# Queries pooled earlier on GpSimd in the first batches, and the first keys turned on TensorE ahead of the first queries

## The chip, the core and the metric

The kernel runs on one core of a Trainium2 chip. The metric is the device time of one execution in microseconds. A core has five engines that run side by side, each through its own list of instructions in order: TensorE (PE, matrix products), VectorE (DVE), ScalarE (ACT), GpSimd (POOL) and SyncE (SP, which here only issues DMA transfers). They meet at semaphores. Before the change three runs took 1130.13, 1131.37 and 1131.44 us, median 1131.37.

## What is computed

The reference has two parts, all in float32. The first is attention for 8 batches of 8 heads over 1152 positions of 64 features, with queries averaged in pairs:

```
q_pool = q.reshape(B, H, S // 2, 2, D).mean(axis=3)      # 576 queries a head
scores = 1/sqrt(D) * q_pool @ k.T                         # 576 x 1152
attn   = exp(scores - rowmax);  attn /= sum(attn) + 1e-9
attn_out = attn @ v
```

The second takes the 4608 rows of 512 features that come out and sends each through one of 8 experts (two products of 512x1024 and 1024x512 with a relu between them), chosen by the largest of 8 gate logits, and scales the result by the gate's probability.

## The kernel before, in words

Attention is worked off in 32 pairs of heads: pair n is head pair hp = n mod 4 of batch b = n div 4 (b and hp both from 0). Each pair has two units, one for each half of its 576 pooled queries. A unit goes through these steps:

- Scores (`scores`, line 631): 9 key chunks, four 64x64 matmuls each, into a bank of PSUM. DVE takes each bank out into a tile `s` (line 635) and keeps the chunk's extreme values (`mx`, reduced at lines 659 and 662, with a small matmul at line 656 between them).
- Exponentials on ACT (line 666), in place in `s`.
- Folds on POOL (`chunk_sum`, line 726): `s` has 9 chunks of 576 columns; POOL adds chunks 0 to 2 and 3 to 5 (1728 columns), adds 6 to 8, and then the third of the three sums to the first (576 columns). So a unit costs POOL two long additions and a short one. The last unit of a batch has one long addition alone (line 722). TensorE sums the folded tiles of a pair's two units with a product against ones (line 716).
- Values (`values`, line 770): products of `s` with the values `vn` into a bank `pa`, taken out by ACT and DVE (lines 776 and 777).

Before a pair's first scores there are its loads and turns (`load_pair`). SP issues the loads at line 490: keys `kp`, queries `qn`, values `vn`, each as four DMAs of 144 KB (128 bytes of an element at a time for keys and queries). POOL adds neighbouring queries, `qp<-qn` (line 520, the pooling). DVE turns the pooled queries into `qT` (line 533, two halves) and the keys into `kT` (line 529, three pieces). There is one `qn` buffer and one `qp` buffer, so the next pair's `qn` load waits until POOL has pooled the one before, and the pooling until DVE has turned the one before. There are two `kp`, three `vn`, four `s` and three `fold` buffers.

The very first pair is different (`first_pair`): its queries and keys are loaded with whole rows, TensorE turns them by products with an identity matrix (`cross_k`, line 589, and `cross_q`, line 595, which pools as it goes), and ACT copies the turned keys and DVE the first half of the turned queries out of PSUM (line 582).

The order of the instructions on each engine is fixed when the program is built. Every step is given to a planner (`Flow`) with an engine, an estimate of its time and a key; the planner runs an event list with one free time for each engine, and takes on each engine the step with the lowest key among those that are ready. A pair's keys start from `key` = 40 times its number. The pooling has `key + K_POOL` with `K_POOL = -28`, a fold `key + K_SUM` with `K_SUM = 25` plus 20 for each half and 20 more. DMAs are steps of the plan as well, with an estimated time from issue to landing (`move`). Once built, an engine keeps to the order whatever really comes late: a step whose data is not there holds all that stands behind it on its engine.

After pair 3's keys and values SP also issues, once, stores that fill scratch memory: `empty_lists`, `gate_weights` and `last_rows` (lines 400 to 412). Attention takes the span up to about 670 us, the experts the rest.

Of the kernel before, what the change touches and what calls it, by code (L numbers as in the profile page):

```python
# [14 lines left out]
ALU = mybir.AluOpType  # L15
# [17 lines left out]
K_POOL = -28  # L33
# [230 lines left out]
def kernel(  # L264
# [170 lines left out]
    def heads(t, b, hp):  # L435
        t = t[b] if isinstance(b, int) else t[bass.ds(b, 1)].rearrange("o h s d -> (o h) s d")
        return t[2 * hp:2 * hp + 2]
# [7 lines left out]
    def turn_ns(n):  # L445
        return 67 + 1.042 * n

    def pool(n):
        return 140 + 2.125 * n
# [10 lines left out]
    def tile_of(o, kind, shape, dt=F32, bufs=None, name=None, pool=None):  # L460
        return hold_of(kind, lambda h: (pool or o.wk).tile(shape, dt, **h.own(name or kind, bufs)))
# [10 lines left out]
    def done(*steps):  # L472
        return [s for s in steps if s is not None]

    def load_pair(o, f, key, b, hp):

        x = Pools()
        x.later, x.late = {}, hp
        opening = not o.exact and b == 0 and hp == 0
        if opening:  # L480
            return first_pair(o, f, key, x)

        kp = tile_of(o, "kp", [P, NQD * NC, BL], bufs=2, pool=o.ld)
        qn = tile_of(o, "qn", [P, NJ, NB, 2, BL], pool=o.ld)
        x.vn = vn = tile_of(o, "vn", [P, 2, NC, D], bufs=3, pool=o.rt)
        qp = tile_of(o, "qp", [P, NJ, NB, BL], pool=o.ld)
        x.kT = kT = tile_of(o, "kT", [P, NC * P], bufs=KT_BUFS, pool=o.kq)
        x.qT = qT = tile_of(o, "qT", [P, NQ], bufs=KT_BUFS, pool=o.kq)

        load = lambda out, src: nc.sync.dma_start(out=out, in_=src)  # L490
        rows = NQD * NC

        def quarters(t, src, n0=0, n1=rows):

            for h in range(2):
                for i in range(D // BL):
                    g = (h * D // BL + i) * BL
                    load(t[g:g + BL, n0:n1], src[h][:, i * BL:(i + 1) * BL].rearrange("(p n) d -> p n d", p=BL)[:, n0:n1])

        def k_part(n0, n1, ns, move, after=()):  # L500
            return f.carry("SP", ns, lambda: quarters(kp.t, heads(k, b, hp), n0, n1), key + K_LOAD, after, [kp], move)

        start = not o.exact and b == 0 and hp == 1

        def q_part(n0, n1, ns, move):
            return f.carry("SP", ns, lambda: quarters(qn.t.rearrange("p j b t d -> p (j b t) d"), heads(q, b, hp), n0, n1),
                    key + K_LOAD, (), [qn], move, 3000 if first and hp == 2 else 0)

        js = [slice(half * NJ // 2, (half + 1) * NJ // 2) for half in range(2)]
        first = not o.exact and b == 0  # L510
        paced = first and hp < 3
        move = 4400 if first else 2600
        k0 = k_part(0, rows, 1900, move, done(not start and o.asked or None))
        cuts = [(0, rows // 2), (rows // 2, rows)] if start else [(0, rows)]
        q0 = [q_part(n0, n1, 1900 // len(cuts), move // len(cuts)) for n0, n1 in cuts]
        vb = heads(v, b, hp).rearrange("h (p b c) d -> b p h (c d)", b=NQD, c=NC)
        x.v = f.carry("SP", 1900, lambda: [load(vn.t[i * BL:(i + 1) * BL].rearrange("p h c d -> p h (c d)"), vb[i]) for i in range(NQD)],
                      key + K_V, done(q0[-1] and q0[-1][9][0]), [vn], 2200 if first else move)
        parts = js if start else [slice(0, NJ)]
        q1 = [f.add("POOL", pool(NJ * QP // len(parts)), lambda j=j: nc.gpsimd.tensor_tensor(  # L520
            qp.t[:, j], qn.t[:, j, :, 0, :], qn.t[:, j, :, 1, :], ALU.add), key + K_POOL, done(got), [qn, qp])
            for j, got in zip(parts, q0)]
        q1 = [q1[0], q1[-1]]
        o.asked = q0[-1] and q0[-1][9][0]
        key += K_PIECE + (START if start else 0)
        x.k, x.q = {}, {}

        def turn_k(c0, n):
            nc.vector.transpose(kT.t.rearrange("p (c b i) -> p b c i", b=NQD, i=BL)[:, :, c0:c0 + n],  # L529
                                kp.t.rearrange("p (b c) d -> p b c d", b=NQD)[:, :, c0:c0 + n])  # L530

        def turn_q(half):
            nc.vector.transpose(qT.t.rearrange("p (j b i) -> p j b i", b=NB, i=BL)[:, js[half]], qp.t[:, js[half]])  # L533

        def turned(half):
            x.q[half] = done(f.add("DVE", turn_ns(HQ), lambda: turn_q(half), key + 7 * half, done(q1[half], paced and o.pace or None), [qT, qp]))
            o.turned.extend(x.q[half])

        turned(0)
        for c0 in range(0, NC, TURN):  # L540
            n = min(TURN, NC - c0)
            e = f.add("DVE", turn_ns(n * P), lambda c0=c0, n=n: turn_k(c0, n), key + 2 + c0 / 2, done(k0, paced and o.pace or None), [kT, kp])
            o.turned.extend(done(e))
            x.k.update((c, done(e)) for c in range(c0, c0 + n))
        turned(1)
        return x

    def first_pair(o, f, key, x):
# [8 lines left out]
        qn = lambda u: flat()[:QP, 2 * NC * D + u * 4 * QP * 2:2 * NC * D + (u + 1) * 4 * QP * 2].rearrange("p (h n d) -> p h n d", h=2, d=D)  # L557
# [5 lines left out]
        def load_q(u, gs, eng):  # L563
            for g in gs:
                eng.dma_start(out=qn(u)[g * BL:(g + 1) * BL].rearrange("p h n d -> p h (n d)"),
                                    in_=heads(q, 0, 0).rearrange("h (i u g n) d -> u g i h (n d)", i=BL, u=2, g=NB)[u, g])
# [3 lines left out]
        q0 = [done(f.carry("SP", 500, lambda: load_q(0, (0,), nc.sync), at + 1, (), [raw], 350),  # L570
                   f.carry("ACT", 900, lambda: load_q(0, range(1, NB), nc.scalar), at + 1, (), [raw], 700))]
# [7 lines left out]
        def turned(fn, ns, n, to, key, after, eng, cost, copy):  # L579
            pt = score_banks(o)  # L580
            t = f.add("PE", ns, lambda: fn(pt.t[:, 0, :n.stop - n.start]), key, after, [pt, raw], COLS)
            made = done(f.add(eng, cost(n.stop - n.start), lambda: copy(to.t[:, n], pt.t[:, 0, :n.stop - n.start]), key, done(t), [pt, to]))
            o.turned.extend(made)
            return made
# [6 lines left out]
        def cross_q(u, to):  # L591
            for m in range(NB):
                for t in range(2):
                    for h, up in enumerate(both):
                        nc.tensor.matmul(to.rearrange("p (g m i) -> p m g i", g=NB, i=BL)[up, m], qn(u)[:, h, 2 * m + t], ident[:QP, :QP],
                                         start=t == 0, stop=t == 1, tile_position=(0, up.start))

        def turn_k(c0, n, at, got, behind=()):
            made = turned(lambda to: cross_k(c0, n, to), 400 * n, slice(c0 * P, (c0 + n) * P), kT, key + at, done(got, *behind), "ACT", act, nc.scalar.copy)
            x.k.update((c, made) for c in range(c0, c0 + n))  # L600

        def turn_q(u, at, got, behind=()):
            side = ("ACT", act, nc.scalar.copy) if u else ("DVE", dve, nc.vector.tensor_copy)
            x.q[u] = turned(lambda to: cross_q(u, to), 1600, slice(u * HQ, (u + 1) * HQ), qT, key + at, [*got, *behind], *side)

        turn_k(0, FIRST, 0, k0[0])
        turn_q(0, -1, q0[0])
        x.later = {1: lambda m: turn_k(FIRST, TURN, 0, k0[1], m), 4: lambda m: turn_k(FIRST + TURN, TURN, 0, k0[1], m),
                   7: lambda m: turn_q(1, 0, q0[1], m)}
        return x  # L610
# [193 lines left out]
    def attend(o, f, key, b, hp, xT, sm, summed):  # L804
        x = load_pair(o, f, key, b, hp)
        outs = []
        end = not o.exact and hp == NHP - 1 and b == B - 1
        for half in range(2):
            at = key + 20 * half
            s, r = scores(o, f, at, x, half, EXPS)  # L810
            summed += chunk_sum(o, f, at + 20, s, r, b, hp, half, sm, summed[-1:])
            outs.append(values(o, f, at + 10 - (40 if end and half else 0), x, s, r, hp, half, xT))
        return done(*outs)
# [592 lines left out]
    with ExitStack() as cm, ExitStack() as units, ExitStack() as pairs:  # L1406
        o, m = open_attention(False, cm, pairs, units), Pools()
# [19 lines left out]
        for b in range(B):  # L1427
# [10 lines left out]
            key = PAIR * (b * NHP + NHP)  # L1438
# [45 lines left out]
    with tc.If(more > 0):  # L1484
        again = nc.values_load(stab[0:1, 1:2], min_val=0, max_val=1,
                               skip_runtime_bounds_check_because="a comparison's result")
        with tc.If(again > 0):
            reset_state()
            empty_lists()
            with ExitStack() as cm:  # L1490
                o = open_attention(True, cm, cm, cm)
# [16 lines left out]
        with ExitStack() as cm:  # L1508
            o, m, f = Pools(), Pools(), Flow()
# [41 lines left out]
```

## Time and profile before

| | |
|---|---|
| median of three runs | 1131.37 us (1130.13 to 1131.44) |
| profiled execution | 1125.42 us, of which its span 1123.6 us |
| granted TensorE clock, mean | 0.999 |
| TensorE busy | 1109.8 us (99%) |
| VectorE busy | 875.9 us (78%) |
| GpSimd busy | 857.6 us (76%) |
| ScalarE busy | 619.7 us (55%) |
| DMA, mean over the span | 141 GB/s |

The profiled execution has 1.82 us around its span. Times in the rows below are counted from the start of the span. A row of the timeline begins with when the instruction (or the first of xN equal ones) started and how long it (or all of them together) took, and ends, where the engine stood idle just before, with that idle time and what ended it, in square brackets.

### The profile page before, as it was taken

Reading aid. Unit: us, or ns where it says so; the run is one execution under the profiler, and the core shown is the slowest. Engines: PE = TensorE matmul, PEld = TensorE weight load, DVE = VectorE, ACT = ScalarE, POOL = GpSimd, SP = SyncE. Lnnn points to the kernel's source line nnn. Section 1 sums busy time; section 2 is a strip of 40 time slices with the busy share of each in tenths; the row PEclk is TensorE's granted clock in tenths of the full one; section 3 lists DMA queues with packets and bytes.
Section 4 is the critical chain, followed back from the end, with each engine's and each line's share of the span. In section 5 each row is a group of like instructions: output and inputs, shape, how many; then the busy total and the mean of one; then the engine's idle time right before and its main releaser. Section 6 shows DMA issues by size and latency. Waiting matters only on the chain.

```text
span 1123.6 us, 32966 instructions
## 1 busy us (share of the span) xinstructions
PE 1109.8 (99%) x13317; PEld 797.1 (71%) x13317; DVE 875.9 (78%) x2244; ACT 619.7 (55%) x835; POOL 857.6 (76%) x488
## 2 busy tenths in 40 slices
PE   9999999999999999999999999999999999999997
PEld 5565565565565565655655558998889989899996
DVE  7898998988989979989989969755555665677761
ACT  3756565666556656566557465544444445555551
POOL 3899999999999899998999854576666655456511
PEclk9999999999999999999999999999999999999999
DMA  9876757537738738637635159865555666577640
GB/s 158 141 139 111 129 86 124 113 66 122 115 66 132 112 64 139 114 66 134 112 63 99 27 169 243 232 188 166 164 174 176 201 192 191 191 233 255 229 158 30
DMA packets 387502, 158.06 MB, mean 141 GB/s; under 512 B 302694, under 2 KB 357762, under 8 KB 387342
## 3 DMA queue, kind: packets, MB, share of 16 engines
q1 hardware_dynamic: 376718, 134.91, 54.4%
q0 software_dynamic: 10464, 20.78, 5.9%
q8 instruction: 106, 1.74, 0.8%
q14 instruction: 54, 0.44, 0.2%
q10 hardware_dynamic: 160, 0.20, 0.1%
HBM read 135.02 MB, written 22.07 MB: 140 GB/s over the span
## 4 chain that ended last, share of the span: by engine, by line
PE 66%; DVE 15%; issue 6%; POOL 5%; DMA 4%; SPq 2%; ACT 0%; POOLq 0%; DVEq 0%; ACTq 0%
PE py L1384 17%; PE ph L1354 16%; PE pa L770 15%; PE st L631 14%; DVE s L635 8%; POOL fold L726 3%; DMA vn<-in_v_dram 2%; SPq L490 2%; DVE kT L529 2%; PE st L716 2%; DVE row L937 1%; PE st L709 1%; POOL qp L520 1%; DVE qT L533 1%; DMA x_runs<-row 1%
## 5 line engine op out<-in xcount | busy, mean ns | idle before, releaser
L666 ACT ACTIVATE s<-s,bias 128x1152 f32<-128x1152 f32 (+1 forms) x320 | 351.3, 1152 | 166.4 <-DVE bias L662 156.7
L635 DVE TENSOR_SCALAR_CACHE_REDUCE s<-st 128x576 f32<-128x576 f32 x576 | 415.1, 748 | 32.4 <-PE st L631 21.7
L631 PE MATMUL st<-qT,kT 64*64 64x288 f32 x4608 | 359.9, 407 | 4.6 <-DVE s L635 2.8
L770 PE MATMUL pa<-s,vn 64*64 64x288 f32 x4608 | 351.4, 404 | 1.0 <-DVE xT L777 0.8
L631 PEld LDWEIGHTS st<-qT,kT 64*64 64x64 f32 x4608 | 166.9, 133 | 121.3 <-DVE s L635 37.3
L770 PEld LDWEIGHTS pa<-s,vn 64*64 64x64 f32 x4608 | 174.6, 133 | 104.3 <-DVE xT L777 10.8
L726 POOL TENSOR_TENSOR fold<-s 128x1728 f32<-128x1728 f32 x55 | 213.0, 3875 | 5.5 <-ACT s L666 3.1
L726 POOL TENSOR_TENSOR fold<-fold,s 128x1728 f32<-128x1728 f32 x55 | 213.0, 3876 | 0.9
L1354 PE MATMUL ph<-xh,w1h 128*128 128x248 f32 (+4 forms) x512 | 155.6, 304 | 0.2 <-DVE hl L1364 0.2
L1354 PE MATMUL ph<-xh,w1l 128*128 128x248 f32 (+4 forms) x512 | 154.6, 302 | 0.0
L1354 PE MATMUL ph<-xl,w1h 128*128 128x248 f32 (+4 forms) x512 | 154.6, 302 | 0.0
L1226 DVE TENSOR_TENSOR w2l<-raw,w2h 128x1024 fp32r<-128x1024 f32 x64 | 78.3, 1223 | 80.6 <-ACT w2h L1311 76.8
L1083 POOL DMA_INDIRECT xr<-x_runs,ix x76 | 97.5, 1283 | 51.6 <-issue 26.0
L1384 PE MATMUL py<-w2h,hh 128*128 128x512 f32 x328 | 128.1, 391 | 0.0
L1384 PE MATMUL py<-w2h,hl 128*128 128x512 f32 x328 | 127.8, 390 | 0.0
L1384 PE MATMUL py<-w2l,hh 128*128 128x512 f32 x328 | 127.8, 390 | 0.0
L1393 POOL DMA_INDIRECT out_dram<-y,rec x41 | 43.9, 1071 | 85.7 <-ACT y L1401 70.3
L1362 ACT ACTIVATE hh<-ph 128x372 fp32r<-128x372 f32 (+4 forms) x100 | 49.3, 493 | 108.2 <-PE ph L1354 108.0
L1354 PEld LDWEIGHTS ph<-xh,w1h 128*128 128x128 f32 x512 | 96.4, 188 | 2.6 <-issue 0.9
L1354 PEld LDWEIGHTS ph<-xl,w1h 128*128 128x128 f32 x512 | 96.4, 188 | 0.7
L1354 PEld LDWEIGHTS ph<-xh,w1l 128*128 128x128 f32 x512 | 96.4, 188 | 0.0
L1364 DVE SCALAR_TENSOR_TENSOR hl<-ph,hh 128x372 fp32r<-128x372 f32 (+4 forms) x100 | 55.6, 556 | 51.1 <-ACT hh L1362 50.8
(230 smaller groups left out, 1339.1 us busy)
## 6 DMA issues: line engine op xcount, KB each, us to landing
raw<-in_moe_w_dram SPq DMA_DIRECT2D x128, 512.0 KB
kp<-in_k_dram SPq DMA_DIRECT2D x124, 144.0 KB
vn<-in_v_dram SPq DMA_DIRECT2D x124, 144.0 KB
qn<-in_q_dram SPq DMA_DIRECT2D x120, 144.0 KB
x_runs<-row SPq DMA_DIRECT2D x96, 99.0 KB
xr<-x_runs,ix POOLq DMA_INDIRECT x76, 4.3
x_runs<-empty SPq DMA_DIRECT2D x4, 297.0 KB
xq<-x_runs,ix POOLq DMA_INDIRECT x52, 3.3
```

The lines of the kernel that those rows point to most:

```text
L631: nc.tensor.matmul(pt.t[to, h, :HQ], x.kT.t[up, c * P + i * D:c * P + (i + 1) * D], x.qT.t[up, cols], start=True, stop=True, tile_position ...
L635: nc.vector.tensor_scalar(s.t[:, c], pt.t[:, :, :HQ], -SCALE, None, op0=ALU.mult, op1=ALU.min, accum_out=mx.t[:, c:c + 1],)
L666: nc.scalar.activation(s.t[:, c0:c0 + n], s.t[:, c0:c0 + n], AF.Exp, bias=bias.t, scale=-1.0)
L726: add = lambda to, a, b: nc.gpsimd.tensor_tensor(to, a, b, ALU.add)
L770: mark.made = nc.tensor.matmul(pa.t[cs, i, :HQ], x.vn.t[up, h, c, :], s.t[up, c, h], start=c == 0, stop=c == NC - 1, tile_position=(up.sta ...
L1083: ins = nc.gpsimd.indirect_dma_start(out=x.xr[i // NQD].t[:, i % NQD, :], out_offset=None, in_=xg, in_offset=bass.IndirectOffsetOnAxis(ap= ...
L1226: (nc.gpsimd if eng == "POOL" else nc.vector).tensor_tensor(lo, raw, hi.bitcast(F32), ALU.subtract)
L1354: mark.made = nc.tensor.matmul(view()[:, i, :], a[:, c, fp], b[:, c, :n], start=c == 0 and k == 0, stop=c == NDC - 1 and k == 2)
L1362: a = f.add("ACT", act(nb * n) - 44, lambda home=home, apart=apart: nc.scalar.activation(home(0), apart(), AF.Relu), at - 20, done(p), [ph ...
L1364: d = f.add("DVE", dve(nb * n), lambda home=home, apart=apart: nc.vector.scalar_tensor_tensor(home(1), apart(), 0.0, home(0).bitcast(F32), ...
L1384: mark.made = nc.tensor.matmul(py.t, blocks(a)[:, c * x.nr + r], b[:, c % 2, :], start=c == 0 and k == 0, stop=c == NFC - 1 and k == 2)
L1393: ins = nc.gpsimd.indirect_dma_start(out=out, out_offset=bass.IndirectOffsetOnAxis(ap=x.re.t.bitcast(I32)[:, r, 0:1], axis=0), in_=y.t, in ...
```

## The change

Two keys are moved; no instruction is added or removed. A pooling's key falls by 32 for head pairs 2 and 3 of batch 0 and head pair 0 of batch 1 (pairs 2, 3 and 4). In the first pair, the first half of the queries goes through TensorE with key +1 in place of -1, the first keys have 0.

```diff
         paced = first and hp < 3
+        sooner = not o.exact and (b == 0 and hp >= 2 or b == 1 and hp == 0)
...
         q1 = [f.add("POOL", pool(NJ * QP // len(parts)), lambda j=j: nc.gpsimd.tensor_tensor(
-            qp.t[:, j], qn.t[:, j, :, 0, :], qn.t[:, j, :, 1, :], ALU.add), key + K_POOL, done(got), [qn, qp])
+            qp.t[:, j], qn.t[:, j, :, 0, :], qn.t[:, j, :, 1, :], ALU.add), key + K_POOL - 32 * sooner, done(got), [qn, qp])
...
         turn_k(0, FIRST, 0, k0[0])
-        turn_q(0, -1, q0[0])
+        turn_q(0, 1, q0[0])
```

What the planner makes of it is seen in the order of the instructions. On POOL, from the pooling of pair 2 on, the order before is this; `qp_0_570`, `qp_0_851` and `qp_0_1142` are the poolings of pairs 2, 3 and 4, `s_2_379` is the second unit of pair 0, `s_3_493` and `s_0_595` are the units of pair 1, and `s_1_733` the first unit of pair 2.

```order
L520 TENSOR_TENSOR qp_0_570<-qn_0_362 128x576
...
L726 TENSOR_TENSOR fold_1_616<-fold_1_616,s_2_379 128x1728
L726 TENSOR_TENSOR fold_2_725<-s_3_493 128x1728
L726 TENSOR_TENSOR fold_1_616<-fold_1_616 128x576
L726 TENSOR_TENSOR fold_2_725<-fold_2_725,s_3_493 128x1728
L520 TENSOR_TENSOR qp_0_851<-qn_0_590 128x576
L726 TENSOR_TENSOR fold_2_725<-fold_2_725 128x576
L726 TENSOR_TENSOR fold_0_901<-s_0_595 128x1728
L726 TENSOR_TENSOR fold_1_954<-s_1_733 128x1728
L726 TENSOR_TENSOR fold_0_901<-fold_0_901,s_0_595 128x1728
...
L520 TENSOR_TENSOR qp_0_1142<-qn_0_881 128x576
```

After the change the same stretch of POOL reads as follows (the poolings of pairs 2, 3 and 4 are `qp_0_570`, `qp_0_725` and `qp_0_953`; the second unit of pair 1 is folded into `fold_0_885`).

```order
L521 TENSOR_TENSOR qp_0_570<-qn_0_362 128x576
...
L727 TENSOR_TENSOR fold_1_616<-fold_1_616,s_2_379 128x1728
L521 TENSOR_TENSOR qp_0_725<-qn_0_590 128x576
L727 TENSOR_TENSOR fold_1_616<-fold_1_616 128x576
L727 TENSOR_TENSOR fold_2_777<-s_3_493 128x1728
L727 TENSOR_TENSOR fold_2_777<-fold_2_777,s_3_493 128x1728
L727 TENSOR_TENSOR fold_0_885<-s_0_595 128x1728
L727 TENSOR_TENSOR fold_2_777<-fold_2_777 128x576
L521 TENSOR_TENSOR qp_0_953<-qn_0_803 128x576
L727 TENSOR_TENSOR fold_0_885<-fold_0_885,s_0_595 128x1728
L727 TENSOR_TENSOR fold_1_1036<-s_1_733 128x1728
```

Pair 2's pooling stays where it was. Pair 3's moves ahead of two long folds and a short one, pair 4's ahead of three long folds and two short ones; the pooling of pair 5 moves ahead of one short fold. From the last unit of batch 0 (line 722) on, POOL's order is the same as before.

On SP, the queue that issues the loads, the order after the scratch stores before the change is the following (`qn_0_881` is pair 4's queries, `qn_0_1164` pair 5's, `kp_0_912` and `vn_1_1023` are pair 4's keys and values).

```order
L412 DMA x_runs_59<-empty_125 576x1x132 x4
L490 DMA qn_0_881<-in_q_dram 32x36x32 x4
L490 DMA kp_0_912<-in_k_dram 32x36x32 x4
L490 DMA vn_1_1023<-in_v_dram 32x2x576 x4
L490 DMA qn_0_1164<-in_q_dram 32x36x32 x4
L490 DMA kp_1_1189<-in_k_dram 32x36x32 x4
```

After the change it is this (`qn_0_803` pair 4's queries, `qn_0_982` pair 5's).

```order
L413 DMA x_runs_59<-empty_125 576x1x132 x4
L491 DMA qn_0_803<-in_q_dram 32x36x32 x4
L491 DMA kp_0_831<-in_k_dram 32x36x32 x4
L491 DMA qn_0_982<-in_q_dram 32x36x32 x4
L491 DMA vn_1_1031<-in_v_dram 32x2x576 x4
L491 DMA kp_1_1058<-in_k_dram 32x36x32 x4
```

Up to pair 4's keys nothing moved on SP: pair 4's queries still stand behind the scratch stores. Pair 5's queries moved ahead of pair 4's values.

On PE, the first products after the warm-up were, before the change:

```order
L1423 MATMUL st_213<-ones 128x512 x2
L595 MATMUL st_232<-ident,s_216 64x3x32 x12
L589 MATMUL st_254<-ident,s_216 64x128 x6
L631 MATMUL st_270<-qT_261,kT_268 64x288 x4
L589 MATMUL st_280<-ident,s_216 64x128 x6
```

After the change they are these, with the queries (line 596 now) behind the first keys (line 590 now).

```order
L1424 MATMUL st_213<-ones 128x512 x2
L590 MATMUL st_232<-ident,s_216 64x128 x6
L596 MATMUL st_248<-ident,s_216 64x3x32 x12
L632 MATMUL st_270<-qT_268,kT_261 64x288 x4
L590 MATMUL st_280<-ident,s_216 64x128 x6
```

The two groups have changed places, and what follows them is the same.

## Rows read from the trace of the kernel before

**Rows 1.** The profile's page, busy time of each engine.

```profile
PE 1109.8 (99%) x13317; PEld 797.1 (71%) x13317; DVE 875.9 (78%) x2244; ACT 619.7 (55%) x835; POOL 857.6 (76%) x488
```

**Rows 2.** Stretches of the span: length, then each engine's busy time (instructions), clock, DMA.

```profile
50.00:100.00 50.00, 48.49 (x800) 30.41 (x800) 42.81 (x125) 29.05 (x31) 50.00 (x19) 1.00 0.63 117
...
110.00:650.00 540.00, 537.35 (x8763) 319.24 (x8755) 488.11 (x1490) 323.12 (x429) 517.83 (x214) 1.00 0.57 99
```

**Rows 3.** Timeline of POOL: start us, us, instruction, [idle before <-releaser].

```profile
33.34 1.40 POOL L520 TENSOR_TENSOR qp<-qn 128x576 f32<-128x576 f32 x1 [2.98 <-DMA qn<-in_q_dram]
...
40.02 3.88 POOL L726 TENSOR_TENSOR fold<-fold,s 128x1728 f32<-128x1728 f32 x1
43.85 3.89 POOL L726 TENSOR_TENSOR fold<-s 128x1728 f32<-128x1728 f32 x1
47.70 1.42 POOL L726 TENSOR_TENSOR fold<-fold 128x576 f32<-128x576 f32 x1
...
52.91 1.42 POOL L520 TENSOR_TENSOR qp<-qn 128x576 f32<-128x576 f32 x1
...
73.69 1.43 POOL L520 TENSOR_TENSOR qp<-qn 128x576 f32<-128x576 f32 x1
...
93.11 1.45 POOL L520 TENSOR_TENSOR qp<-qn 128x576 f32<-128x576 f32 x1
...
102.13 1.45 POOL L520 TENSOR_TENSOR qp<-qn 128x576 f32<-128x576 f32 x1
```

**Rows 4.** Timeline of DVE, the turns of pairs 2, 3, 5 and 6.

```profile
34.78 0.48 DVE L533 STREAM_TRANSPOSE qT<-qp 128x288 f32<-128x288 f32 x1 [1.02 <-POOL qp L520]
...
54.36 0.84 DVE L533 STREAM_TRANSPOSE qT<-qp 128x288 f32<-128x288 f32 x2 [1.47 <-POOL qp L520]
...
94.59 0.84 DVE L533 STREAM_TRANSPOSE qT<-qp 128x288 f32<-128x288 f32 x2
...
103.89 0.47 DVE L533 STREAM_TRANSPOSE qT<-qp 128x288 f32<-128x288 f32 x1
```

**Rows 5.** Timeline of PE, the waits between 50 and 80 us.

```profile
55.91 2.07 PE L631 MATMUL st<-qT,kT 64*64 64x288 f32 x24 [0.95 <-DVE s L635]
...
76.39 1.69 PE L770 MATMUL pa<-s,vn 64*64 64x288 f32 x24 [0.46 <-DVE xT L777]
```

**Rows 6.** Timeline of SP, issues of loads and scratch stores (time spent issuing).

```profile
36.17 4.49 SPq L490 DMA_DIRECT2D qn<-in_q_dram  x4
...
52.88 4.13 SPq L412 DMA_DIRECT2D x_runs<-empty  x4
57.11 4.95 SPq L490 DMA_DIRECT2D qn<-in_q_dram  x4
```

**Rows 7.** The last of such a group of issues alone, in three narrow windows.

```profile
16.64 0.50 SPq L490 DMA_DIRECT2D qn<-in_q_dram  x1
...
39.61 1.05 SPq L490 DMA_DIRECT2D qn<-in_q_dram  x1
...
61.24 0.81 SPq L490 DMA_DIRECT2D qn<-in_q_dram  x1
```

**Rows 8.** The chain of waits, pair 2's queries; POOL's timeline, pair 1's second half.

```profile
27.16 6.05 DMA qn<-in_q_dram
...
19.74 0.80 POOL L520 TENSOR_TENSOR qp<-qn 128x288 f32<-128x288 f32 x1 [1.85 <-DMA qn<-in_q_dram]
```

**Rows 9.** Timeline of PE at the start, and of DVE's copy of the queries.

```profile
5.21 1.21 PE L595 MATMUL st<-ident,s 96*64 96x96 f32 x24 [0.32 <-DMA s<-in_q_dram]
6.22 0.86 PE L589 MATMUL st<-ident,s 128*64 128x128 f32 x12
7.64 0.71 PE L631 MATMUL st<-qT,kT 64*64 64x288 f32 x8 [0.57 <-ACT kT L582]
...
6.45 0.46 DVE L582 COPY qT<-st 128x288 f32<-128x288 f32 x1 [1.85 <-PE st L595]
```

## The prediction

> **What bounds the kernel now.** I read the page's busy line first: TensorE 99%, GpSimd 76%, VectorE 78% [rows 1]. A share over the whole span hides stages, so I asked for stretches next. From 50 to 100 us, where the moved poolings lie, POOL is busy 50.00 of 50.00 us and PE 48.49; from 110 to 650 us PE is busy 537.35 of 540 us and POOL 517.83 [rows 2]. The reader is to see two things there. In the stretch of the change POOL has no gap at all. And after 110 us PE has only 2.65 us of gaps, so time that PE loses before 110 us can hardly be won back.
>
> Then the timelines of POOL, DVE and PE, to see who waits for whom. DVE waits for a pooling before its turns of pairs 2 and 3 (1.02 and 1.47 us) and comes just in time for pairs 5 and 6 [rows 4]: pair 5's pooling starts at 93.11 and takes 1.45, so it ends at 94.56, and DVE's turn starts at 94.59; pair 6's ends at 102.13 + 1.45 = 103.58, and its turn starts at 103.89 [rows 3, 4]. So through this stretch DVE, and PE behind it, run at POOL's pace, with 0.0 to 0.3 us to spare. PE's own gaps there are 0.95 us at 55.91 and 0.46 us at 76.39 [rows 5]; these are what the change can win.
>
> Last the timeline of SP, for the loads. SP issues pair 4's queries from 57.11 on, directly behind the scratch stores (52.88 + 4.13 = 57.01) [rows 6]. POOL had pooled pair 3 by 52.91 + 1.42 = 54.33 [rows 3], so the buffer was free 2.8 us before: it is SP's own queue that sets when these queries are loaded, not POOL. The last of the four DMAs is issued at 61.24 [rows 7]. Before the change this did no harm, because POOL came to pair 4's pooling at 73.69 [rows 3].
>
> **The change, part by part.**
>
> *First keys ahead of the first queries.* Now PE turns the queries at 5.21, after 0.32 us of waiting for their load, then the keys from 6.22 for 0.86, and the first scores start at 7.64, after ACT's copy of the keys [rows 9]. If the keys have landed by 4.89 (5.21 - 0.32), their turn runs from 4.89 to about 5.75, the queries' 1.21 us end at 6.96 or up to 0.2 earlier (the two turns overlapped by 0.2 before: 1.21 against a distance of 1.01), DVE's copy takes 0.46, and the scores start at about 7.3 to 7.45, 0.2 to 0.3 us sooner. If the keys land only when PE now gets to them (6.22), the same steps give 8.6 to 8.75, 1.0 to 1.1 us later. I take 0.2 sooner. Either way the end doesn't feel it. POOL's pooling of pair 2 starts at 33.34 on the landing of its queries, after 2.98 us of idle time, and DVE waits 1.02 us for it [rows 3, 4]; that load is paced by SP. A sooner start lengthens this wait, a later one eats it. Price: 0; where the cover of 1.02 us isn't enough, 0.1 us.
>
> *Pair 2's pooling* stays at its place: 0.
>
> *Pair 3's pooling* moves ahead of two long folds and a short one. POOL ends the fold before it at 43.85 [rows 3]. The queries' last DMA is issued at 39.61 [rows 7]. What lies between such an issue and the pooling is 6.05 us for pair 2 (27.16 to 33.21) and 19.74 - 16.64 = 3.10 us for pair 1 [rows 7, 8]. Those are my bounds for the landing; I take their middle, 4.6 us, since both loads stand in a queue that SP keeps filled. So the pooling starts at 44.2 (43.85 to 45.7) in place of 52.91. DVE's 1.47 us and PE's 0.95 us go [rows 4, 5]. What is late next?
>
> *Pair 4's pooling* moves ahead of three long folds and two short ones. POOL's steps follow each other a little closer than their busy times (43.85 to 47.70 is 3.85 for a row of 3.89 [rows 3]), so I count 3.85 for a long fold and 1.38 for a short one or a pooling. From 43.85, without any wait, POOL does pair 3's pooling, a short fold, three long folds and a short fold: 3 x 1.38 + 3 x 3.85 = 15.7, and asks for pair 4's queries at 59.5. Their last DMA isn't issued before 61.24 [rows 7]. With 4.6 us the queries are there at 65.8. POOL stands still 65.8 - 59.5 = **6.3 us** (counted with the short wait at pair 3, which lies inside it), in a stretch where it had no idle time [rows 2]. With the bounds 3.10 and 6.05 it is 4.8 and 7.8 us.
>
> The Trainium skill has a rule for what lies between issue and landing: on the page "DMA: Bandwidth & Descriptors", section "Anatomy of one DMA — SWDGE (gpsimd) path", about 2.0 us plus the bytes at 436 GB/s. It is fitted there for DMAs that GpSimd issues, so for SP's it is an estimate from that page: 2.3 us for 144 KB, pair 4's queries at 63.6, a stop of 4.1 us. The two landings that the trace shows are longer, 3.10 and 6.05 us [rows 7, 8], so by the trace the rule is too short for loads in a filled queue; by it the sum below would be 3.8 instead of 6.0.
>
> *Who pays for the stop.* Behind the waiting pooling on POOL stand the folds of pair 1's second unit and of pair 2, and so the row sums on PE (line 716), which PE takes in order. DVE waits at pair 4's turn and holds the takes of scores behind it, so PE runs out of free banks. PE is ahead then by the gaps that went (0.95, later 0.46), and loses that lead. From there all three go at POOL's pace. Pair 5's pooling is ahead of one short fold, which gives 1.4 us back for a moment; the fold is then owed. From line 722 on the order on POOL is as before, and pair 6's pooling comes 6.3 us later, at 108.4. Before, DVE had 0.3 us to spare there. So DVE and PE go on 6.3 - 0.3 = **6.0 us** late (4.5 to 7.5 with the bounds). The gains of 0.95 and 0.46 are not taken off again: they only brought PE sooner to the place where it waits. After 110 us PE has 2.65 us of gaps in all [rows 2], so at the very most that much comes back; I take 0, since a uniform delay also delays what these gaps wait for.
>
> *SP.* Pair 5's queries now stand ahead of pair 4's values and wait for pair 4's pooling to end (65.8 + 1.4 = 67.2), so those values are issued at about 72 (67.2 + 4.95 for four such DMAs [rows 6]) in place of about 67 (57.11 + 2 x 4.95). They are used only behind pair 4's scores and exponentials, which begin with its turn at 67. Price: 0, up to 1 us if the values should be late.
>
> **The sum.** 0 + 0 + 6.0: the profiled execution's 1125.42 us would become 1131.4 us. The median of the runs is 1131.37 us, 5.95 above that execution; the sum adds to either, so I forecast 1131.37 + 6.0 = **1137.4 us**.
>
> **Rivals.**
>
> 1. *Not slower: the queries are there when POOL asks.* Place: pair 4's pooling. If its four DMAs landed before 59.5, POOL wouldn't stop, and the gaps of 0.95 and 0.46 us with the 0.2 us at the start would be won: -1.6 us, 1129.8. For it: SP only needs `qn` free, and now it is free at 45.6. Against: it was free before SP got there already, and SP's order up to these DMAs is unchanged, with the last issue at 61.24. It decides from a landing before 59.5; the likeliest way is that SP issues everything faster than in this one trace.
>
> 2. *The stop is there, but shorter, or partly won back.* With the shorter landing, 3.10 us after the issue, PE ends 4.5 us late. If PE's 2.65 us of later gaps took up part of 4.5 to 6.0, 1.8 to 3.3 us are left. Time: 1133.2 to 1135.9. For it: no row shows the landing of just these DMAs, and pair 1's was short. The Trainium skill's rule named above stands on this side, with 3.8 us. Against: the load most like this one in size and place took 6.05, and PE's gaps lie spread over 540 us.
>
> 3. *The stop is longer*, over 7.5 us, because the queries stand behind the scratch stores, or pair 4's values come late: 1139 to 1140.
>
> That the change does less than its words is true in part: of three poolings two move.
>
> **How the numbers follow.** What a measurement can tell here from no change is 0.2%, 2.3 us. Forecast (4.5 to 7.5 late): 0.66. Rival 2: 0.17, most of it over 2.3 us (0.15). Rival 3: 0.06. Rival 1: 0.08, and all of its 1.6 us lie within 0.2%. 0.03 is left for a gain that I don't see. So slower 0.66 + 0.15 + 0.06 = 0.87, same 0.08 + 0.02 = 0.10, faster 0.03. Range: from rival 2's low end, 1131.37 + 1.8 = 1133.2, rounded down to 1133.0, to 1131.37 + 7.5 = 1138.9 and 1 us for late values, 1139.9; outside lie rival 1 and half of rival 3.
>
> **What would show it right or wrong.** Right: on POOL an idle time of 4 to 8 us ended by the DMA of `qn`, before a pooling near 66 us; none over 2 us before pair 3's pooling near 44 us; DVE's turn of pair 4 after a wait for POOL of about 6 us; PE with a new gap of some 5 us near 68 us, the gaps at 55.9 and 76.4 gone; pair 6's turn at about 110; from there the same rows as before, about 6 us later. Scores starting at 7.3 to 7.5, and pair 2's pooling still near 33.3. Wrong: pair 4's pooling near 60 without a wait, or PE's rows at 150 us less than 3 us late although POOL stopped.

## The result, and the profile after

The changed kernel takes 1136.08 us (median of six runs, 1135.37 to 1139.29) against 1131.38 for the kernel before (six runs beside them, 1129.1 to 1132.57): a ratio of 1.0051, 95% interval 1.0037 to 1.0065. It is 4.7 to 5.8 us slower, by the medians and by the ratio.

The busy line of the page, which answers to [rows 1], hardly tells: TensorE has 98% in place of 99%.

```profile
PE 1113.8 (98%) x13317; PEld 795.9 (70%) x13317; DVE 877.1 (77%) x2244; ACT 618.8 (55%) x835; POOL 854.8 (75%) x488
```

The same two stretches as in [rows 2] do. From 50 to 100 us POOL lost 5.50 of its 50.00 us and PE 48.49 - 45.55 = 2.94 (counted in products it is more: 727 in place of 800), and the mean granted clock is 0.97 there. From 110 to 650 us little differs: whatever was lost was lost before.

```profile
50.00:100.00 50.00, 45.55 (x727) 25.50 (x720) 39.01 (x113) 29.34 (x32) 44.50 (x18) 0.97 0.58 105
110.00:650.00 540.00, 536.20 (x8713) 318.48 (x8709) 485.47 (x1481) 318.34 (x430) 516.62 (x212) 1.00 0.60 100
```

POOL's timeline, to be laid beside [rows 3] (all lines of the kernel are one higher now):

```profile
32.48 1.41 POOL L521 TENSOR_TENSOR qp<-qn 128x576 f32<-128x576 f32 x1 [1.91 <-DMA qn<-in_q_dram]
...
43.81 1.42 POOL L521 TENSOR_TENSOR qp<-qn 128x576 f32<-128x576 f32 x1 [0.76 <-DVE s L636]
...
58.17 1.41 POOL L727 TENSOR_TENSOR fold<-fold 128x576 f32<-128x576 f32 x1
65.00 1.40 POOL L521 TENSOR_TENSOR qp<-qn 128x576 f32<-128x576 f32 x1 [5.42 <-DMA qn<-in_q_dram]
66.35 3.85 POOL L727 TENSOR_TENSOR fold<-fold,s 128x1728 f32<-128x1728 f32 x1
...
107.64 1.41 POOL L521 TENSOR_TENSOR qp<-qn 128x576 f32<-128x576 f32 x1
```

Pair 3's pooling came to 43.81 (52.91 before), pair 4's only to 65.00 (73.69), and ahead of it POOL stood still for 5.42 us, until the DMA of `qn` had landed. Pair 6's pooling, ahead of which POOL has now done the same work as before, starts at 107.64 in place of 102.13: 5.51 us late. That is the stop of 5.42 and the 0.76 of waiting ahead of pair 3's pooling, less the 0.86 by which this execution was ahead at pair 2's (32.48 in place of 33.34), to 0.2 us.

DVE's turns of pairs 3, 4 and 6 ([rows 4] has pair 6 at 103.89, so 5.19 us late), and PE's waits between 40 and 110 us with the row behind the longest, in place of the two of [rows 5]:

```profile
45.27 0.48 DVE L534 STREAM_TRANSPOSE qT<-qp 128x288 f32<-128x288 f32 x1 [1.40 <-POOL qp L521]
...
66.43 0.48 DVE L534 STREAM_TRANSPOSE qT<-qp 128x288 f32<-128x288 f32 x1 [5.47 <-POOL qp L521]
...
109.08 0.48 DVE L534 STREAM_TRANSPOSE qT<-qp 128x288 f32<-128x288 f32 x1 [0.18 <-POOL qp L521]
```

```profile
46.46 0.71 PE L632 MATMUL st<-qT,kT 64*64 64x288 f32 x8 [0.88 <-DVE s L636]
...
67.62 3.69 PE L632 MATMUL st<-qT,kT 64*64 64x288 f32 x32 [4.30 <-DVE s L636]
71.13 2.12 PE L771 MATMUL pa<-s,vn 64*64 64x288 f32 x32
...
100.24 1.39 PE L632 MATMUL st<-qT,kT 64*64 64x288 f32 x16 [0.34 <-DVE s L636]
```

PE's row names DVE as what ended its gap: PE had no free bank left, and DVE, which empties the banks, stood at pair 4's turn. DVE itself had waited for the pooling, and that for the DMA. Of this chain only the last link, the landing of the DMA, is the cause. On SP the stores and pair 4's queries follow each other as in [rows 6], and pair 5's queries now stand ahead of pair 4's values; the third row is the last issue of pair 4's queries alone ([rows 7]):

```profile
52.02 3.79 SPq L412 DMA_DIRECT2D x_runs<-empty  x4
55.91 5.30 SPq L490 DMA_DIRECT2D qn<-in_q_dram  x4
...
60.18 1.03 SPq L490 DMA_DIRECT2D qn<-in_q_dram  x1
...
66.49 3.70 SPq L490 DMA_DIRECT2D qn<-in_q_dram  x4
70.28 2.21 SPq L490 DMA_DIRECT2D vn<-in_v_dram  x4
```

One thing on reading the two traces against each other. The spans differ by 10.7 us (1134.3 and 1123.6), twice the timed difference. The profiled execution of before was 6 us under its own median. The 5.2 to 5.5 us that are there at 110 us belong to the change; most of the rest comes behind 600 us, and the profiled executions differ there without the change too: that of the kernel called `stores_moved` below has pair 6's pooling 0.16 us later than before, and yet its span is 2.6 us longer.

### The profile page after: what moved, and what is told of

It reads as the page before. It is cut to its first block, busy times and chain, and to the rows that moved or that the text cites. A ratio compares the mean times of both kernels' runs of the same rounds, so it can differ in the third digit from the quotient of the medians.

```text
span 1134.3 us, 32967 instructions
## 1 busy us (share of the span) xinstructions
PE 1113.8 (98%) x13317; PEld 795.9 (70%) x13317; DVE 877.1 (77%) x2244; ACT 618.8 (55%) x835; POOL 854.8 (75%) x488
## 4 chain that ended last, share of the span: by engine, by line
PE 69%; DVE 16%; issue 7%; DMA 3%; POOL 2%; SPq 2%; ACT 0%; POOLq 0%; DVEq 0%; ACTq 0%
PE py L1385 16%; PE pa L771 16%; PE st L632 16%; PE ph L1355 15%; DVE s L636 9%; PE st L717 2%; DVE kT L530 2%; DVE row L938 2%; DMA vn<-in_v_dram 2%; PE st L710 1%; SPq L490 1%; POOL fold L727 1%; DVE lw L861 1%; DVE st L874 0%; POOL out_dram L1394 0%
## 5 line engine op out<-in xcount | busy, mean ns | idle before, releaser
L727 POOL TENSOR_TENSOR fold<-s 128x1728 f32<-128x1728 f32 x55 | 213.0, 3873 | 12.3 <-ACT s L667 10.7
L1084 POOL DMA_INDIRECT xr<-x_runs,ix x76 | 90.8, 1194 | 51.7 <-issue 25.6
L1084 POOL DMA_INDIRECT xq<-x_runs,ix x52 | 60.0, 1154 | 47.4 <-PE py L1385 24.6
```

The costliest lines, as they stand in the source:

```text
L727: add = lambda to, a, b: nc.gpsimd.tensor_tensor(to, a, b, ALU.add)
L1084: ins = nc.gpsimd.indirect_dma_start(out=x.xr[i // NQD].t[:, i % NQD, :], out_offset=None, in_=xg, in_offset=bass.IndirectOffsetOnAxis(ap= ...
```

## The experiments

Theory 1 is that of the prediction: POOL, which must keep its order, stands still at pair 4's pooling until queries land that SP issues behind the scratch stores, and that stop is the loss. Theory 2: poolings ahead of folds cost time by themselves, wherever the loads land. Theory 3: the new order of the first turns costs it. Each kernel was timed beside the kernel before on the same chip. The three chips give before 1129.01 us (`pools_only`, `turn_only`, `pair3_only`, `late7000`), 1129.78 (`late5000`, `stores_moved`, `big_stores`, `big_stores_before`) and 1125.43 (`pair4_only` and the three called `cut`).

### One part of the change at a time

All diffs are against the changed kernel, where nothing else is said. `pools_only` and `turn_only` halve the change (the second is built from the kernel before):

```diff
-        turn_q(0, 1, q0[0])     # pools_only
+        turn_q(0, -1, q0[0])
...
-        turn_q(0, -1, q0[0])    # turn_only, against the kernel before
+        turn_q(0, 1, q0[0])
```

> The change without the new order of the first turns (queries before keys again); the three earlier poolings stay. Theory 1 (POOL stands still until pair 4's queries land): pair 4's pooling again near 65 us after 5 to 6 us of waiting for the DMA of qn, and the kernel as slow as the changed one, 5 to 6 us over before (ratio 1.004 to 1.005). Theory 3 (the cost comes from the start, where the scores began 0.23 us later): no more than 0.5 us over before, ratio 1.000.

> Only the new order of the first turns; the poolings stand where they stood. Theory 1: the first scores begin near 7.9 us, pair 2's pooling still near 33 us, pair 4's near 73.7 us without a wait, and the time within 0.5 us of before (ratio 1.000). Theory 3: 4 to 6 us over before (ratio 1.004 to 1.005).

`pair3_only` and `pair4_only` keep the new order of the first turns and leave out one of the two poolings that move:

```diff
-        sooner = not o.exact and (b == 0 and hp >= 2 or b == 1 and hp == 0)
+        sooner = not o.exact and b == 0 and hp >= 2           # pair3_only
+        sooner = not o.exact and b == 1 and hp == 0           # pair4_only
```

> The new order of the first turns and the earlier poolings of pairs 2 and 3; pair 4's pooling keeps its low rank. Theory 1: POOL comes to pair 4's pooling after 68 us, the queries have landed (65.0 us in the changed kernel), so no wait over 1 us, and the time is 0 to 1.4 us under before (the 0.95 and 0.46 us of PE's gaps), ratio 0.999 to 1.000. Theory 2 (poolings ahead of folds cost by themselves, wherever the loads land): 2 to 5 us over before, ratio 1.002 to 1.004.

> The new order of the first turns and the earlier poolings of pairs 2 and 4; pair 3's pooling keeps its low rank (near 52.9 us). Pair 4's pooling then stands behind one long fold more than in the changed kernel. Theory 1: POOL asks near 63.3 us (54.3 + 1.4 + 2 x 3.85), the queries land near 65, stop 1.5 to 2 us, pair 6's pooling 1.5 to 2.7 us later than before and the time the same amount over before (ratio 1.001 to 1.0025). Rival (pair 4's earlier pooling costs its full 5 us whoever stands ahead of it): ratio 1.004 to 1.005.

Measured: `pools_only` 1134.88 us, ratio 1.0049 (1.0036 to 1.0062), as slow as the whole change; `turn_only` 1128.98, 0.9994 (0.9983 to 1.0005). Theory 3 falls. `pair3_only` 1129.87, 1.0010 (1.0001 to 1.0020): not the gain of up to 1.4 us that I allowed, and far from theory 2's 2 to 5 us. `pair4_only` 1128.0, 1.0026 (1.0015 to 1.0037), 2.6 to 2.9 us.

Pair 4's pooling in the timelines of POOL, in `pools_only`, `turn_only` and `pair3_only`, one fence each: the wait is there in the slow one alone.

```profile
65.90 1.39 POOL L521 TENSOR_TENSOR qp<-qn 128x576 f32<-128x576 f32 x1 [5.76 <-DMA qn<-in_q_dram]
```

```profile
73.45 1.45 POOL L520 TENSOR_TENSOR qp<-qn 128x576 f32<-128x576 f32 x1
```

```profile
71.72 1.41 POOL L521 TENSOR_TENSOR qp<-qn 128x576 f32<-128x576 f32 x1
```

In `pair4_only` the time came out near what was expected, but its trace doesn't show why. There the queries had landed when POOL asked, and the profiled execution, 1124.87 us, is the shortest of its twelve:

```profile
63.96 1.41 POOL L521 TENSOR_TENSOR qp<-qn 128x576 f32<-128x576 f32 x1
76.86 1.41 POOL L521 TENSOR_TENSOR qp<-qn 128x576 f32<-128x576 f32 x1 [1.07 <-PE st L632]
```

In the five profiled executions with a wait there and the same stores ahead (the changed kernel, `pools_only`, `late5000`, `cut_ahead`, `cut_behind`) the pooling starts between 64.43 and 65.90, all later than here; with such a landing POOL would have stopped for 0.5 to 1.9 us in this order too. Whether the other eleven runs had that stop, or whether the other order behind it costs (pair 5's pooling has moved up to 76.86, and waits there), stays open. What the times show is that pair 3's pooling alone costs next to nothing, pair 4's alone about half of the loss, and both together all of it; with both, POOL asks at 59.58 (the end of the fold from 58.17), over 4 us sooner than here.

### The same earlier pooling, asked for later

These keep the whole change and tell the planner a later landing for pair 4's queries alone, so that it puts one or two long folds more ahead of that pooling (`late5000` is shown; `late7000` has 7000):

```diff
-   key + K_LOAD, (), [qn], move, 3000 if first and hp == 2 else 0)
+   key + K_LOAD, (), [qn], move, 3000 if first and hp == 2 else 5000 if not o.exact and b == 1 and hp == 0 else 0)
```

> The changed kernel with pair 4's queries taken by the planner to land 5000 ns later: one long fold more stands ahead of their pooling. Theory 1 with the loss equal to what is left of the stop: POOL asks at 59.6 + 3.85 = 63.4 us, landing at 65.0, stop 1.6 us, time 0.5 to 1.8 us over before (ratio 1.0005 to 1.0015). Rival (a stop there costs the same whatever its length, because PE falls out of step): 4 to 6 us over before (ratio 1.004 to 1.005).

> The changed kernel with one number more for its planner: pair 4's queries are taken to land 7000 ns later, so that the plan puts two long folds ahead of their pooling. Theory 1: POOL asks for them at 59.6 + 2 x 3.85 = 67.3 us, after their landing at 65.0, so it doesn't wait, DVE's turn of pair 4 comes near 69 us, and the time is 0 to 1.4 us under before (ratio 0.999 to 1.000). Theory 2: still 4 to 6 us over before (ratio 1.004 to 1.005), without a wait for qn.

`late7000`: 1129.49 us, 1.0003 (0.9995 to 1.0012). Pair 4's pooling doesn't wait, and pair 6's starts at 103.08:

```profile
68.07 1.41 POOL L521 TENSOR_TENSOR qp<-qn 128x576 f32<-128x576 f32 x1
...
103.08 1.42 POOL L521 TENSOR_TENSOR qp<-qn 128x576 f32<-128x576 f32 x1
```

So the later pooling is the cheaper one: started 3.07 us later than in the changed kernel, it takes 4.2 to 5.4 us off the time (4.70 over before to 0.48 by the medians, 0.51% to 0.03% by the ratios). Theory 2 falls with it, since here too it stands ahead of folds that it stood behind before.

`late5000`: 1132.37 us, 1.0024 (1.0014 to 1.0033), that is 2.6 to 2.7 us, more than the 0.5 to 1.8 expected. The stop has the size that was worked out (1.49 us for 1.6); PE's gap is longer than the stop. POOL's row, and then PE's:

```profile
65.81 1.40 POOL L521 TENSOR_TENSOR qp<-qn 128x576 f32<-128x576 f32 x1 [1.49 <-DMA qn<-in_q_dram]
```

```profile
68.43 0.72 PE L632 MATMUL st<-qT,kT 64*64 64x288 f32 x8 [2.77 <-DVE s L636]
```

PE ran out of free banks at 65.66 (68.43 - 2.77), just ahead of the pooling, and got the next one 2.62 us behind the pooling's start (68.43 - 65.81), when POOL had pooled, DVE had turned and then taken out one bank of scores. In the changed kernel it is 2.62 us as well (67.62 - 65.00). So what PE loses isn't POOL's stop: it runs from when PE has no bank left to 2.62 us behind the pooling's start, and these 2.77 us are close to the time.

### The load made earlier and later

`stores_moved` is the changed kernel with the four scratch stores issued behind pair 5's keys; the instructions on POOL, DVE, PE and ACT stand as in the changed kernel. `big_stores` doubles the bytes of the same stores, and `big_stores_before` does so in the kernel before.

```diff
+  [last_rows() for _ in range(not o.exact and b == 1 and hp == 1)] +        # stores_moved: ahead of pair 5's values
-  f.carry("SP", 2000, last_rows, 100, outs, [], 3400)
+  f.carry("SP", 2000, lambda: None, 100, outs, [], 3400)
...
-  planes[g, NT - NQ:NT] ... j=NJ                                            # big_stores
+  planes[g, NT - 2 * NQ:NT] ... j=2 * NJ
```

> The changed kernel with its four scratch stores issued behind pair 5's keys in place of ahead of pair 4's queries; the order on POOL, DVE, PE and ACT is the changed kernel's. Theory 1, with the stores as what makes the queries late: SP issues pair 4's queries from 52.0 to 57.3 us in place of 55.9 to 61.2, they land near 61 us, POOL asks at 59.6 and stops for 0 to 1.5 us, and the time is 1.5 us under to 1.5 us over before (ratio 0.999 to 1.001). Rival (the load itself takes that long there, stores or not): landing again near 65 us, 5 us over before (ratio 1.004 to 1.005).

> The changed kernel with scratch stores of twice the bytes (2.38 MB in place of 1.19; the rows above the last are also written). Theory 1: 1.19 MB more at the 255 GB/s of that stretch is 4.7 us, so pair 4's queries land near 69.7 us, POOL stops for about 10 us in place of 5.4, and the time is 9 to 11 us over before (ratio 1.008 to 1.010). Rival (landing set by something else): landing near 65 us, 5 us over before (ratio 1.004 to 1.005).

> The kernel before with the same doubled scratch stores. Theory 1: pair 4's queries land near 70 us, still ahead of their pooling at 73.7, so nothing waits: within 1 us of before (ratio 0.999 to 1.001). Rival (the bytes cost the kernel by themselves): 4 to 5 us over before (ratio 1.004).

`stores_moved`: 1129.4 us, 1.0000 (0.9991 to 1.0010). All of the loss is gone without a step moved on any computing engine. SP's rows, then POOL's:

```profile
52.23 4.03 SPq L490 DMA_DIRECT2D qn<-in_q_dram  x4
...
72.82 4.02 SPq L412 DMA_DIRECT2D x_runs<-empty  x4
```

```profile
59.60 1.39 POOL L521 TENSOR_TENSOR qp<-qn 128x576 f32<-128x576 f32 x1
```

POOL comes to the pooling at 59.60, the 59.5 of the prediction, and the queries are there. They were issued 3.68 us sooner than in the changed kernel (52.23 in place of 55.91) and were there at least 5.40 sooner (59.60 in place of 65.00), so the stores ahead delay their issue and, for the rest, their transfer.

`big_stores`: 1141.36 us, 1.0098 (1.0081 to 1.0114), 11.1 to 11.6 us. The stores take SP 6.25 us to issue in place of 3.79, the queries behind them 7.50 in place of 5.30, and POOL's stop is 10.78 us:

```profile
52.84 6.25 SPq L412 DMA_DIRECT2D x_runs<-empty  x4
59.19 7.50 SPq L490 DMA_DIRECT2D qn<-in_q_dram  x4
```

```profile
70.94 1.39 POOL L521 TENSOR_TENSOR qp<-qn 128x576 f32<-128x576 f32 x1 [10.78 <-DMA qn<-in_q_dram]
```

`big_stores_before`: 1128.86 us, 0.9994 (0.9984 to 1.0005). The same bytes cost nothing where the pooling stands late:

```profile
73.25 1.41 POOL L520 TENSOR_TENSOR qp<-qn 128x576 f32<-128x576 f32 x1
```

Laid side by side, the start of pair 6's pooling against its 102.13 before, and the timed difference of medians (`pair4_only`, 2.57, can't stand here: its pair 6 is pooled earlier in POOL's order, at 96.27):

| kernel | pair 6's pooling | later by | time over before |
|---|---|---|---|
| turn_only | 101.86 | -0.27 | -0.03 |
| big_stores_before | 101.69 | -0.44 | -0.92 |
| pair3_only | 101.52 | -0.61 | 0.86 |
| stores_moved | 102.29 | 0.16 | -0.38 |
| late7000 | 103.08 | 0.95 | 0.48 |
| late5000 | 104.78 | 2.65 | 2.59 |
| the change | 107.64 | 5.51 | 4.70 |
| pools_only | 108.54 | 6.41 | 5.87 |
| big_stores | 113.54 | 11.41 | 11.58 |

In these nine, one row of one profiled execution foretells the median of other executions to within 1.5 us, over a range of 12. What is late there stays late.

### Who pays behind the stop

The prediction let DVE and PE follow POOL's pace behind the stop. To see whether POOL is what holds them, one long fold was cut from 1728 to 288 columns, ahead of pair 4's pooling or right behind it, and for comparison in the kernel before:

```diff
-  lambda: add(u.t, u.t, s.t[:, 6:9])
+  lambda: add(u.t[:, 0, 0], u.t[:, 0, 0], s.t[:, 6, 0]) if not o.exact and b == 0 and (hp, half) == (1, 0)  # cut_ahead; (1, 1) in the others
+          else add(u.t, u.t, s.t[:, 6:9])
```

> The changed kernel with one fold ahead of pair 4's pooling (the adding one of pair 1's first unit, at 50.50 us) cut from 1728 to 288 columns, which leaves a part of that pair's row sums out; every other instruction stands where it stood. It takes about 0.8 us in place of 3.87, 3.1 us less work for POOL. Theory 1: the queries still land near 65 us, POOL only stops for 3.1 us more (8.5 in place of 5.4), pair 6's pooling stays 5 to 6 us later than before, and the time is that of the changed kernel (ratio to before 1.004 to 1.005). Rival (POOL's amount of work in this stretch sets the end, not the landing): 3 us won, ratio 1.0015 to 1.0025.

> The changed kernel with the same cut in the fold right behind pair 4's pooling (the adding one of pair 1's second unit, at 66.35 us), 3.1 us less work for POOL behind the stop; part of that pair's row sums is left out. Theory 1 with POOL as what sets the pace behind the stop: the stop is again 5 to 6 us, and 2.5 to 3.1 us are won behind it: pair 6's pooling 2.4 to 3 us later than before, ratio to before 1.002 to 1.003. Rival (behind the stop PE and DVE set the pace, with as much to catch up as POOL): POOL waits later for them instead, no more than 1 us won, ratio 1.004 to 1.005.

> The kernel before with the same cut as the last (the adding fold of pair 1's second unit, near 67 us there); part of that pair's row sums is left out. If POOL alone sets the pace between 50 and 110 us, 3.1 us are won (ratio 0.997). If PE, busy for 48.49 of 50 us there, is the bound right behind it, no more than the 1.5 us of its gaps are won (ratio 0.9985 to 1.000), and an earlier pooling had no more than that to win either.

The times of these three can't be used, which I had not foreseen: the missing part of the row sums changes which expert a row is sent to, and the experts' stage comes to 45, 49 and 49 tiles of rows in place of 41 (1245.21, 1357.51 and 1352.83 us). The stretch up to 110 us lies before that and can be read.

`cut_ahead`: 3.07 us less work for POOL ahead of the stop, the stop 7.58 us in place of 5.42 (and 0.57 more idle ahead of the next fold), pair 6's pooling 5.60 late in place of 5.51. Work saved ahead of the stop was worth nothing.

```profile
50.91 0.80 POOL L727 TENSOR_TENSOR fold<-fold,s 128x288 f32<-128x288 f32 x1
...
65.11 1.40 POOL L521 TENSOR_TENSOR qp<-qn 128x576 f32<-128x576 f32 x1 [7.58 <-DMA qn<-in_q_dram]
...
107.73 1.43 POOL L521 TENSOR_TENSOR qp<-qn 128x576 f32<-128x576 f32 x1
```

`cut_behind`: here POOL does win, pair 6's pooling is at 104.04, 3.6 us sooner than in the changed kernel. But DVE turns pair 6 at 108.10 in place of 109.08, only 0.98 sooner, and 0.57 of that is the landing of pair 4's queries, which was sooner here (64.43). Its rows of POOL and DVE, and then the busy times from 68 to 110 us in the changed kernel and in `cut_behind`:

```profile
104.04 1.42 POOL L521 TENSOR_TENSOR qp<-qn 128x576 f32<-128x576 f32 x1
```

```profile
108.10 0.47 DVE L534 STREAM_TRANSPOSE qT<-qp 128x288 f32<-128x288 f32 x1
```

```profile
68.00:110.00 42.00, 41.66 (x668) 23.63 (x664) 36.36 (x103) 21.85 (x23) 42.00 (x16) 0.97 0.55 90
```

```profile
68.00:110.00 42.00, 42.00 (x672) 23.70 (x672) 36.59 (x105) 22.44 (x24) 41.70 (x16) 0.96 0.55 94
```

Behind the stop both engines are full: POOL 42.00 of 42, PE 41.66. With work taken from POOL, PE has no gap at all any more, and all that DVE's turn of pair 6 gains is 0.4 us. The rival of that expectation holds: PE and DVE are late by themselves, as late as POOL.

`cut_before` can't tell the same for the kernel before. In the stretch from 50 to 100 us PE fills up to 49.96 of 50 us, and POOL begins to wait (2.33 us for ACT's exponentials at 75.30).

```profile
50.00:100.00 50.00, 49.96 (x833) 31.91 (x828) 44.88 (x131) 32.02 (x35) 47.67 (x20) 1.00 0.60 112
```

But this execution came late into the stretch: its first 24 products behind the warm-up took 2.19 us in place of 1.21 [rows 9], and DVE's turn of pair 2 started at 37.60 in place of 34.78 [rows 4]. Its turns of pairs 2 and 6:

```profile
37.60 0.48 DVE L533 STREAM_TRANSPOSE qT<-qp 128x288 f32<-128x288 f32 x1
...
104.56 0.47 DVE L533 STREAM_TRANSPOSE qT<-qp 128x288 f32<-128x288 f32 x1
```

So 2.82 us of lateness shrank to 0.67 (104.56 in place of 103.89), and which part of the full PE is due to the late start, and which to the cut, isn't shown. It does show that the gaps of [rows 2], 50 - 48.49 = 1.5 us, are no strict bound: between 50 and 100 us PE did 33 products more than before (833 and 800), some 2.0 us of work at 0.06 us each, while its busy time rose by 1.47. A row of PE's busy time can hide waits, as [rows 5] have it: 24 products of one shape take 2.07 us in one row and 1.69 in the other.

Nothing of this was won by the earlier poolings. `stores_moved` and `late7000`, the two versions in which they wait for little or nothing, are level with the kernel before, and no version was faster than it by more than the measurement can tell. PE's gaps have moved rather than gone. `stores_moved` has three between 40 and 110 us, together 1.27 us, where [rows 5] have 0.95 and 0.46, together 1.41:

```profile
46.47 0.71 PE L632 MATMUL st<-qT,kT 64*64 64x288 f32 x8 [0.55 <-DVE s L636]
...
65.19 0.71 PE L632 MATMUL st<-qT,kT 64*64 64x288 f32 x8 [0.40 <-DVE s L636]
...
94.88 1.39 PE L632 MATMUL st<-qT,kT 64*64 64x288 f32 x16 [0.32 <-DVE s L636]
```

## Why the prediction was right, point by point

The direction, the place and the mechanism of the stop were right, and 1136.08 is 1.3 us under the 1137.4 forecast. One part of the account, who holds PE behind the stop, was not. By its steps:

- *When POOL asks for pair 4's queries.* Worked out 59.5 from 43.85 and the spacing of the folds. In the changed kernel the short fold from 58.17 ends at 59.58; in `stores_moved` the pooling starts at 59.60. Right.
- *When they land.* Worked out 65.8 as the last issue, 61.24, plus 4.6, the middle of 3.10 and 6.05 [rows 7, 8]. Measured: last issue 60.18, pooling 65.00, so 4.8 us between them. The middle was right to 0.2 us; SP was 1.1 us quicker in this execution, which makes the stop 5.42 in place of 6.3. This is the term that was mis-sized. By the rule that the prediction took from the Trainium skill, "DMA: Bandwidth & Descriptors", section "Anatomy of one DMA — SWDGE (gpsimd) path", the queries would by estimate have been there at 60.18 + 2.3 = 62.5. The trace has 65.00, so the rule is too short for this load, behind four stores of 297 KB.
- *What sets the landing.* The prediction named SP's queue, with the scratch stores ahead. Shown from both sides: moved away, the stop is gone; doubled, it is 10.78 us.
- *Who pays.* Predicted: DVE goes on later by the stop less 0.3, and nothing is won back. Measured: 5.42 us of stop, DVE's turn of pair 6 5.19 late, the timed loss 4.7 to 5.8. The sum held. That PE runs out of free banks while DVE stands at the turn was right too: it does so at 63.32 (67.62 - 4.30). But from there the prediction had DVE and PE follow POOL's pace, and `cut_behind` shows that they don't need POOL to be late: with 3.6 us taken off POOL's lateness, DVE's turn of pair 6 came only 0.98 sooner. PE's own account is a gap of 4.30 us, and behind it 32 products (scores) in 3.69 us, where 32 of the same shape right behind them take 2.12. Together 5.87 us, less the 0.86 by which this execution was ahead at pair 2's pooling: about 5.0, as late as POOL. The prediction took only POOL's lateness, and that PE's came out the same was luck. Nor can the 1.57 us between those two rows simply be put down to the lower clock that is told of below: the 32 products fill four banks, and DVE, which was busy without a gap from 66.43 on, took from 66.83 to 70.54 to empty four. It first waited for PE at 73.89:

```profile
73.89 0.76 DVE L636 TENSOR_SCALAR_CACHE_REDUCE s<-st 128x576 f32<-128x576 f32 x1 [0.39 <-PE st L632]
```

- *What comes back later.* Predicted: 0, with at most the 2.65 us of PE's gaps "after 110 us". [rows 2] end at 650, so the cap was misread: from 650 to 1123.6 us PE has another 473.60 - 466.65 = 6.95 us of gaps. The 0 held; the loss by the medians is about what was there at 110 us.
- *Pair 3's pooling* came at 43.81 (forecast 44.2), after a wait of 0.76 us. Its row names DVE's take for it; in `pair3_only` and `stores_moved` the same pooling waits 0.64 and 0.31 us for the DMA of `qn`. Wrong was that DVE's wait of 1.47 us and PE's gap of 0.95 would go: they came sooner, at 45.27 (1.40) and 46.46 (0.88). So Rival 1 was wrong in giving 1.6 us for the case that nothing stops: `stores_moved` is that case, and is level.
- *The start.* Forecast: scores 0.2 us sooner. Measured: 0.23 later, at 7.87 against 7.64 [rows 9]. I gave the keys' turn the 0.86 us that it took as the second of the two; as the first it takes 1.24, and the queries' then 1.16. The price of 0 held all the same: pair 2's pooling still waits 1.91 us for its load, and `turn_only` is level.

```profile
4.98 1.24 PE L590 MATMUL st<-ident,s 128*64 128x128 f32 x12
6.05 1.16 PE L596 MATMUL st<-ident,s 96*64 96x96 f32 x24
7.87 0.72 PE L632 MATMUL st<-qT,kT 64*64 64x288 f32 x8 [0.66 <-DVE qT L583]
```

- *SP.* Pair 4's values were issued from 70.28 (forecast about 72), behind pair 5's queries, and PE's only wait from there to 110 us is 0.34 us, for DVE. Price 0, right.

## What to carry to other kernels

Before a step is moved up on an engine that keeps its order, compare the time at which the engine will now ask with the time at which the data lands, and read the landing from the queue of the engine that issues the load: here a transfer nobody waits for (the scratch stores) stood ahead in it, harmless for as long as the reader came late. A planner that takes a load to land sooner than it does will make exactly this mistake; mending the plan's number (`late7000`) or the queue (`stores_moved`) each took the whole loss away. And weigh what there is to win against the risk: the gaps that could be seen in the full engine were 1.5 us, the versions that stop nowhere won none of it, and the stop cost 5.

## What the runs showed of the hardware

TensorE's granted clock fell at the stop. Before the change it stayed at 1.00 all through this stretch [rows 2]. In the changed kernel, where PE stood still for 4.30 us up to 67.62, it is half (1.2 of 2.4 GHz) from about 67.2 to 70.6 us; the column behind POOL's busy time is the clock:

```profile
66.00:68.00 2.00, 0.38 (x4) 0.30 (x8) 1.57 (x4) 0.03 (x1) 2.00 (x2) 0.80 1.03 160
68.00:70.00 2.00, 2.00 (x20) 0.84 (x16) 2.00 (x7) 0.00 (x0) 2.00 (x1) 0.50 1.05 152
70.00:72.00 2.00, 2.00 (x32) 0.98 (x28) 2.00 (x7) 0.00 (x0) 2.00 (x2) 0.84 1.07 143
```

The clock's records have it at half for 3.41 us there, as in `cut_ahead` (PE's gap 4.00 us) and `cut_behind` (4.12), for 6.83 in `pools_only` (4.66) and for 10.24 in `big_stores` (9.66). In `late5000`, with a gap of 2.77 us, it stayed at 1.00. I had not reckoned with it. What it cost isn't shown: DVE is full in these rows too (2.00 of 2.00 from 68 to 72 us), so PE would have waited for banks at the full clock as well.
